# An output projection by Strassen's seven half products, and a small product in half-height tiles, in a fused attention and FFN kernel

## The chip, the cores and the metric

The kernel runs on one core of a Trainium2 chip. A core has TensorE (PE in the profile; its weight loads are PEld), VectorE (DVE), ScalarE (ACT), GpSimd (POOL), SyncE (SP, which issues every DMA of this kernel) and 16 DMA engines. The metric is the device time of one launch in microseconds (us), lower is better.

## The reference

Eight batches of x (8 heads, 512 tokens, 64 wide) attend to a state of 32 rows per head, and the state attends to x. Both results go through a two-layer network:

```python
xread = softmax(x @ state.T * scale) @ state          # 512 rows a batch
sread = softmax(state @ x.T * scale) @ x              # 32 rows a batch
x = concatenate([xread, sread], axis=2)               # 544 rows a batch, 512 wide
h = x @ w_in                                          # 512 -> 2048
g = h - tanh(h)
out = g @ w_out                                       # 2048 -> 512
```

## The kernel before

Names used below: a *chunk* is one batch's 512 token rows (chunks 0 to 7); chunk 8 is the 256 state rows of all batches together. The 2048 hidden columns are 16 blocks f of 128.

**Split products.** Every fp32 operand is kept as two rounded parts. `split` (L92) makes them: ScalarE copies the value into a rounded `hi`, VectorE subtracts to get `lo`. A product is then three matmuls: hi·hi, hi·lo, lo·hi.

**Hidden layer.** x itself never meets w_in: for each batch the kernel forms m = state @ w_in and multiplies the attention weights aT by it. `Chunk.hidden` makes one block f of 512 tokens: six matmuls (L392 to L394) into a PSUM bank of `ps_h`, which has two. `finish` applies tanh (ScalarE), then h - tanh (VectorE, one input in PSUM), which frees the bank, then `split` into a `g` tile.

**Output.** `Chunk.output` adds block f to four PSUM banks (`ps_o`, one for each 128 tokens), three matmuls of 512 columns each (L430 to L432): 12 matmuls for each f, 192 for each chunk. The weights w_out stay in on-chip memory as `wo`, all 16 blocks split. `hidden` runs two blocks (`LAG`) ahead of `output`, so a chunk is a strict alternation of 6 and 12 matmuls.

**Where m comes from.** For batches 0 and 1 `m_first_two` makes it. For batches 2 to 7 `m_units` does, beside the chunks: group g = 0 is batches 2 to 5, g = 1 batches 6 and 7. For each of 8 pairs of heads it splits the 64 rows of w_in of each head with a ScalarE copy and a VectorE subtract of 64 partitions (L186, L187), stacking hi and lo on top of each other so that one full-height matmul does two of the three terms. A head then takes two matmuls in g = 0 (L194, L195) and one in g = 1. The result goes to device memory and is loaded back (`load_m`) and split, 1024 columns at a time, when a chunk needs it.

**Beside it.** The attention of batch b runs as nine *units* (a generator), the last four of them the state read. Lists of step numbers say after which step which unit is emitted. A planner with a timeline model orders each engine's queue; each engine then executes its queue strictly in order. `tc.issue_after(x)` puts what is emitted inside it behind x on x's engine. A step is one (chunk, f).

**The start.** w_in and w_out come as 64-bit words and are converted on VectorE and ScalarE in chunk 0 (`Weight.steps`, L124 to L128).

Of the kernel before, what the change touches and what calls it, by code (L numbers as in the profile page):

```python
# [19 lines left out]
P = 128  # L20
# [13 lines left out]
@with_exitstack  # L34
def attention_ffn(ctx: ExitStack, tc: tile.TileContext, xT, xn, bd, bh, sp, sm, sl, win, wout, xout, sout):

# [17 lines left out]

    PB = int('3')
    WB = int('2')
# [4 lines left out]
    OB = int('2')  # L61
    RB = int('2')
    GB = int('3')
    TB = int('3')
    CB = int('2')
    RRB = int('1')
    PTB = int('2')
    ident = cpool.tile([P, P], F32, name="ident")
    make_identity(nc, ident)
    wo = cpool.tile([P, NFF, 2, DM], F32R, name="wo")  # L70
    sr = [cpool.tile([P, DM], F32, name=f"sr{g}") for g in range(2)]
# [15 lines left out]
    def twins(name, shape, dtype):  # L87
        return pool.tile(shape, dtype, tag="twins", name=name)

    raws = itertools.cycle([parts] * PB + [twins] * 2)  # L90

    def split(hi, lo, src, sub=None):  # L92

        nc.scalar.copy(hi, src)  # L94
        return (sub or nc.vector).tensor_sub(lo, src, hi)  # L95

    class Weight:
# [17 lines left out]
        def steps(self, dst):  # L115

            if self.src.dtype == F32:
                return [lambda: None] * 3 + [lambda: nc.gpsimd.tensor_copy(dst, self.raw)]
            low, high = self.raw[:, :, 0], self.raw[:, :, 1]
            u, i = dst.bitcast(U32), dst.bitcast(I32)  # L120
            r = pool.tile([P, 512], I32, tag="cr", name=f"{self.name}r", bufs=CB)
            return [

                lambda: nc.vector.tensor_scalar(u, high, 3, 0x3FFFFFFF, ALU.logical_shift_left, ALU.bitwise_and),  # L124
                lambda: nc.vector.scalar_tensor_tensor(u, high, 0xC0000000, u, ALU.bitwise_and, ALU.bitwise_or),  # L125

                lambda: nc.scalar.activation(r, low, AF.Copy, scale=2.0**-29),
                lambda: nc.vector.tensor_add(i, i, r),  # L128
            ]
# [18 lines left out]
    def second(q):  # L148
        if q < 2:
            return pool.tile([P, 2, 512], F32, tag="stage", name=f"mr1{q}", bufs=SB)  # L150
        return pool.tile([P, 2, 512], F32, tag=f"mr1{q}", name=f"mr1{q}", bufs=1)

# [12 lines left out]
    def m_units(g):  # L165
# [12 lines left out]
        for q in range(NQ):  # L178
            for k in range(2):
                w = pool.tile([P, 2, 512], F32, tag="wf", name=f"w1{g}{q}{k}", bufs=WB)  # L180
                nc.sync.dma_start(w, wf[q][:, 2 * k : 2 * k + 2])
                for c in range(2):
                    p = 2 * k + c

                    t = twins(f"wst{g}{q}{p}", [P, 2, 512], F32R)
                    split(t[0:64, 0], t[64:128, 0], w[0:64, c], WSUB)  # L186
                    split(t[64:128, 1], t[0:64, 1], w[64:128, c], WSUB)  # L187
                    hs = slice(2 * c, 2 * c + 2)
                    stage = pool.tile([P, 2, 512], F32, tag="stage", name=f"st{g}{q}{p}", bufs=SB)
                    for e in range(2):  # L190
                        h = 2 * p + e
                        ps = bank(ps_a, f"mps{g}{q}{h}")
                        if g == 0:
                            nc.tensor.matmul(ps, s[:, 1, h], t[:, e], start=True, stop=False)  # L194
                        nc.tensor.matmul(ps, s[:, 0, h], t[:, e], start=(g == 1), stop=True)  # L195
                        nc.scalar.copy(stage[:, e], ps)  # L196
# [38 lines left out]
    def convert_wout(f, part):  # L235
        w = pool.tile([P, 512], F32, tag="wor", name=f"wor{f}", bufs=RB)
        part.convert(w)
        split(wo[:, f, 0], wo[:, f, 1], w)


    def attention(b, aT):
# [34 lines left out]
        for hf in range(2):  # L276
            if b < LONE:
                scores(hf)
            ps = pss[hf]
            s = pool.tile([P, 512], F32, tag=f"s{b}{hf}" if b < EARLY_S else "s", name=f"s{b}{hf}", bufs=1 if b < EARLY_S else 2)  # L280
            nc.scalar.copy(s, ps)
# [26 lines left out]

    late = {}

# [59 lines left out]
    class Chunk:  # L370
# [9 lines left out]
        def hidden(self, f):  # L380
# [7 lines left out]
            for k in range(nk):  # L388
# [4 lines left out]
                nc.tensor.matmul(ps, mhi[k][:, cols], alo[:, k], start=False, stop=False)  # L393
                nc.tensor.matmul(ps, mlo[k][:, cols], ahi[:, k], start=False, stop=(k == nk - 1))  # L394
            self.finish(f, ps)

        def finish(self, f, ps):
            i, n = self.i, self.n
            t = pool.tile([P, 512], F32, tag="t", name=f"t{i}_{f}", bufs=TB)[:, :n]
            tanhs.append((nc.scalar.activation(t, ps, AF.Tanh).ins, nc.vector.tensor_sub(t, ps, t).ins))  # L400
# [26 lines left out]
        def add(self, f, t):  # L427
            g, o = self.g[f], self.o[t]
            tok = slice(t * P, t * P + P)
            nc.tensor.matmul(o, g[:, 0, tok], wo[:, f, 0], start=(f == 0), stop=False)  # L430
            nc.tensor.matmul(o, g[:, 0, tok], wo[:, f, 1], start=False, stop=False)  # L431
            return nc.tensor.matmul(o, g[:, 1, tok], wo[:, f, 0], start=False, stop=(f == NFF - 1)).ins  # L432

# [93 lines left out]
    def step(op):  # L527
# [7 lines left out]
        elif k == "c":  # L535
            ss[j] = pool.tile([P, 512], F32, tag=f"s0{j}", name=f"s0{j}", bufs=1)
            o(nc.scalar.copy(ss[j], sps_ps[j]))
# [113 lines left out]
    if "att0" in SCH:  # L651
        a2 = SCH.pop("att0")
        D0["att"]["1"] = [x for x in a2]
    D0.update(SCH)
    convs = iter([(1, 2), (1, 3)] + [(q, p) for q in (2, 3) for p in range(4)])
    pairs = iter([(1, 2), (1, 3)] + [(q, p) for q in (2, 3) for p in range(4)])
    wo_it = iter(range(1, NFF))
    for i in range(B + 1):
        for f in range(NFF):
# [10 lines left out]
            if nf < NFF:  # L670
                if nf % 4 == 0:
                    chunks[i].prepare(nf // 4)
                chunks[i].hidden(nf)
            elif i + 1 <= B:
                if nf == NFF:
                    if i + 1 == B:
                        turn_sread()
                    chunks[i + 1].prepare(0)
                chunks[i + 1].hidden(nf - NFF)
            for _ in range(D0["pair"].count(st)):  # L680
                m_first_two(*next(pairs))

            with ExitStack() as gates:
                if st < GATED:
                    for x in tanhs[st]:
                        gates.enter_context(tc.issue_after(x))
                advance(a0, D0["a0"].count(st))
                advance(late1, D0["r1"].count(st))
                for b in range(1, B):
                    n = D0["att"][str(b)].count(st)  # L690
                    if n:
                        if b not in atts:
                            atts[b] = new_attention(b)
                        advance(atts[b], n)
                for g in range(2):
                    advance(m1[g], D0[f"m{g}"].count(st))
            chunks[i].output(f)

# [48 lines left out]
```

## Time and profile before

| | |
|---|---|
| median of 3 runs | 683.47 us (683.39 to 683.52) |
| profiled execution | span 681.6 us from first to last instruction; its own launch time isn't given, the median stands 1.9 us above its span |
| PE busy | 97% of the span |
| VectorE, ScalarE, GpSimd busy | 67%, 56%, 1% |
| moved by DMA | 95.05 MB, mean 139 GB/s |
| first stores of chunk 0 | 130 us |

The span is from the first to the last instruction of one profiled execution. Busy time of PE counts a matmul from its start to its modelled end; matmuls overlap, so the distance between two starts is what one costs. A row of the timeline is start, duration, engine, line, operation, output<-input, shape.

### The profile page before, as it was taken

The page shows a single profiled execution, that of the slowest core. Times are in us where ns is not written, and L with a number is a line of the kernel's source. Part 1 is how long each engine was busy: PE and PEld are TensorE (multiplying, and loading weights), DVE is VectorE, ACT ScalarE, POOL GpSimd, SP SyncE. Part 2 cuts the span into 40 slices and gives each one's busy share as a digit, 9 for nine tenths or more (in the row PEclk, how much of TensorE's full clock was granted, in tenths as well). Part 3 has the DMA queues.
Part 4 walks back from the last instruction along what each step waited for, and adds up shares of the span by engine and source line. Part 5 has one row for each costly group of instructions (what it writes and reads, how often), then busy time and mean ns, then how long its engine had stood idle before and what let it go on. Part 6 is the DMA issues. An engine that isn't in the chain of part 4 may idle for free.

```text
span 681.6 us, 9389 instructions
## 1 busy us (share of the span) xinstructions
PE 657.8 (97%) x3458; PEld 518.4 (76%) x3458; DVE 457.4 (67%) x805; ACT 378.5 (56%) x667; POOL 3.8 (1%) x9
## 2 busy tenths in 40 slices
PE   5888989999999999999999999999999999999997
PEld 2555666788788878787888777887878788888896
DVE  5988999864966469756966488637854687434442
ACT  3878866866756546756756464635433354333342
POOL 2000000000000000000000000000000000000000
PEclk9789999999999999999999999999999999999999
DMA  8779840555536642735445333653241312001310
GB/s 297 202 277 332 279 154 18 174 154 149 189 94 190 167 158 67 243 95 183 129 155 156 124 128 110 200 186 128 93 162 54 124 37 100 21 14 44 129 32 31
DMA packets 43694, 95.05 MB, mean 139 GB/s; under 512 B 5888, under 2 KB 11264, under 8 KB 43648
## 3 DMA queue, kind: packets, MB, share of 16 engines
q1 hardware_dynamic: 43648, 94.46, 43.1%
q8 instruction: 27, 0.44, 0.3%
q14 instruction: 19, 0.16, 0.1%
HBM read 64.55 MB, written 29.88 MB: 139 GB/s over the span
## 4 chain that ended last, share of the span: by engine, by line
PE 81%; DVE 11%; DMA 4%; ACT 1%; issue 1%; SPq 0%; ACTq 0%; DVEq 0%
PE ops L430 16%; PE ops L432 16%; PE ops L431 16%; PE hps L392 8%; PE hps L393 8%; PE hps L394 8%; PE mps L195 2%; DVE t L400 1%; PE rps L346 1%; PE sps L270 1%; DVE wor L125 1%; PE pps L336 1%; DVE g L95 1%; DMA w01d<-in_win 1%; DMA wo2d<-in_wout 1%
## 5 line engine op out<-in xcount | busy, mean ns | idle before, releaser
L431 PE MATMUL ops<-wo,g 128*128 128x512 f32 x544 | 213.7, 393 | 4.5 <-DVE wo L95 4.5
L430 PE MATMUL ops<-wo,g 128*128 128x512 f32 x544 | 207.0, 395 | 0.6 <-ACT wo L94 0.5
L432 PE MATMUL ops<-wo,g 128*128 128x512 f32 x544 | 205.6, 391 | 0.0
L400 DVE TENSOR_TENSOR t<-hps,t 128x512 f32<-128x512 f32 (+1 forms) x142 | 93.7, 661 | 95.8 <-ACT t L400 95.1
L400 ACT ACTIVATE t<-hps 128x512 f32<-128x512 f32 (+1 forms) x142 | 81.6, 575 | 133.8 <-PE hps L394 130.0
L94 ACT CAST g<-t 128x512 fp32r<-128x512 f32 (+1 forms) x142 | 84.8, 598 | 73.7 <-DVE t L400 54.4
L431 PEld LDWEIGHTS ops<-wo,g 128*128 128x128 f32 x544 | 102.2, 188 | 28.8 <-DVE wo L95 7.5
L95 DVE TENSOR_TENSOR g<-t,g 128x512 fp32r<-128x512 f32 (+1 forms) x142 | 93.6, 660 | 45.0 <-ACT g L94 43.5
L430 PEld LDWEIGHTS ops<-wo,g 128*128 128x128 f32 x544 | 102.5, 189 | 27.9 <-ACT wo L94 3.0
L432 PEld LDWEIGHTS ops<-wo,g 128*128 128x128 f32 x544 | 102.0, 188 | 23.4 <-issue 1.3
L392 PE MATMUL hps<-aT,m 128*128 128x512 f32 x248 | 99.8, 403 | 1.2 <-DVE t L400 1.0
L394 PE MATMUL hps<-aT,m 128*128 128x512 f32 x248 | 96.6, 391 | 0.6 <-DVE m L95 0.5
L393 PE MATMUL hps<-aT,m 128*128 128x512 f32 x248 | 97.0, 391 | 0.0
L392 PEld LDWEIGHTS hps<-aT,m 128*128 128x128 f32 x248 | 46.6, 188 | 15.1 <-DVE t L400 2.2
L394 PEld LDWEIGHTS hps<-aT,m 128*128 128x128 f32 x248 | 46.6, 188 | 11.2 <-DVE m L95 1.5
L393 PEld LDWEIGHTS hps<-aT,m 128*128 128x128 f32 x248 | 46.6, 188 | 10.1 <-issue 1.0
L95 DVE TENSOR_TENSOR wst<-w,wst 64x512 fp32r<-64x512 f32 x64 | 43.9, 686 | 13.9 <-ACT wst L94 12.1
L196 ACT COPY st<-mps 128x512 f32<-128x512 f32 x64 | 36.3, 588 | 15.7 <-PE mps L195 14.1
L95 DVE TENSOR_TENSOR m<-mr,m 128x1024 fp32r<-128x1024 f32 x31 | 37.9, 1223 | 8.0 <-ACT m L94 7.8
L94 ACT CAST wst<-w 64x512 fp32r<-64x512 f32 x64 | 39.7, 620 | 0.8
L94 ACT CAST m<-mr 128x1024 fp32r<-128x1024 f32 x31 | 32.3, 1045 | 3.5 <-DMA mr<-md 2.8
L195 PE MATMUL mps<-wst,sms 128*128 128x512 f32 x64 | 24.9, 395 | 0.0
(215 smaller groups left out, 584.1 us busy)
## 6 DMA issues: line engine op xcount, KB each, us to landing
md<-st SPq DMA_DIRECT2D x128, 128.0 KB, 2.2
mr<-md SPq DMA_DIRECT2D x24, 512.0 KB, 4.0
xT<-in_xT SPq DMA_DIRECT2D x16, 512.0 KB, 4.1
w<-wf SPq DMA_DIRECT2D x16, 512.0 KB, 4.3
out_x<-ob SPq DMA_DIRECT2D x32, 256.0 KB, 2.1
xn<-in_xn SPq DMA_DIRECT2D x16, 512.0 KB, 3.5
wn<-wf SPq DMA_DIRECT2D x8, 512.0 KB, 4.1
ml<-md SPq DMA_DIRECT2D x8, 512.0 KB, 3.8
```

The costliest lines, as they stand in the source:

```text
L94: nc.scalar.copy(hi, src)
L95: return (sub or nc.vector).tensor_sub(lo, src, hi)
L125: lambda: nc.vector.scalar_tensor_tensor(u, high, 0xC0000000, u, ALU.bitwise_and, ALU.bitwise_or),
L195: nc.tensor.matmul(ps, s[:, 0, h], t[:, e], start=(g == 1), stop=True)
L196: nc.scalar.copy(stage[:, e], ps)
L392: nc.tensor.matmul(ps, mhi[k][:, cols], ahi[:, k], start=(k == 0), stop=False)
L393: nc.tensor.matmul(ps, mhi[k][:, cols], alo[:, k], start=False, stop=False)
L394: nc.tensor.matmul(ps, mlo[k][:, cols], ahi[:, k], start=False, stop=(k == nk - 1))
L400: tanhs.append((nc.scalar.activation(t, ps, AF.Tanh).ins, nc.vector.tensor_sub(t, ps, t).ins))
L430: nc.tensor.matmul(o, g[:, 0, tok], wo[:, f, 0], start=(f == 0), stop=False)
L431: nc.tensor.matmul(o, g[:, 0, tok], wo[:, f, 1], start=False, stop=False)
L432: return nc.tensor.matmul(o, g[:, 1, tok], wo[:, f, 0], start=False, stop=(f == NFF - 1)).ins
```

## The change

**Output of chunks 2 to 7.** They are taken in three pairs (2,3), (4,5), (6,7), and a new class `Pair` replaces `output` for them. Token rows a and b, even and odd f, and the two 256-column halves of w_out make a 2x2 by 2x2 block product; it is done with seven half products (m1 to m7 in the order of `ORDER`) and sums of blocks. Each half product has four steps j of 12 matmuls (weights: a 128x128 piece of w_out, moving: 512 tokens), so a pair takes 28 steps. The output comes out transposed and is stored to a new tensor `tout`.

- **Weights.** After chunk 0 and 1 `wo` isn't kept: `keep_row` writes its 16 blocks to device memory, `mix_rows` forms four sums of blocks on GpSimd, splits them and writes them too. `Pair.load` fetches the 512 KB for each step again: 84 loads. `load_rows` brings the 16 blocks back for chunk 8.
- **Operands.** h - tanh is kept unsplit in a tile `G`. Before a step `Pair.split` splits 1024 columns of it. `hidden_done` forms two sums for each j, on GpSimd for j 0 to 2 and on VectorE for j = 3. `Pair.split` adds one GpSimd subtraction for each step of m5 and m6.
- **Order.** For the first pair the hidden blocks of chunk 2 come four in a row between steps (ticks "H" and "P"), then those of chunk 3; in the other pairs first two H to one P. Then four P (m6), then 16 P, each followed by one H of the next chunk, except in the last pair, where they follow each other.
- **Sums.** `close` copies finished banks out (ScalarE) or adds a copy to them (VectorE).

**m of batches 2 to 7.** `m_units` splits both heads of a pair in one copy and one subtract of 128 partitions, and multiplies each head in a tile of 64 rows of the array, the two heads in turn: three terms a head in g = 0, two in g = 1.

**Around it.** Buffer counts and the lists of steps change (`ASIDE`, `SIDES`): attention 2 and m_units g = 0 sit in steps 15 to 27, eight `mix_rows` in steps 17 to 30.

```diff
+    def big(name, shape, dtype):
+        return pool.tile(shape, dtype, tag="big", name=name, bufs=BIG)   # BIG=16
...
 def m_units
-                    split(t[0:64, 0], t[64:128, 0], w[0:64, c], WSUB)
-                    split(t[64:128, 1], t[0:64, 1], w[64:128, c], WSUB)
+                    split(t[:, 0], t[:, 1], w[:, c])
...
+                    pss = [bank(ps_a, f"mps{g}{q}{2 * p + e}") for e in range(2)]
+                    terms = [(0, 0), (0, 1)] + [(1, 0)] * (g == 0)
+                    for n, (x, y) in enumerate(terms):
+                        for e in range(2):
+                            rows = slice(64 * e, 64 * e + 64)
+                            nc.tensor.matmul(
+                                pss[e], s[rows, x, 2 * p + e], t[rows, y], start=(n == 0), stop=(n == len(terms) - 1)
+                            )
...
 Chunk.finish
+            if 2 <= i < B:
+                if f % 4 < 2:
+                    self.g[f // 4, f % 2] = big(f"G{i}_{f}", [P, 2, 512], F32)
+                g = self.g[f // 4, f % 2][:, f % 4 // 2]
+                main(nc.scalar.activation(t, ps, AF.Tanh), nc.vector.tensor_sub(g, ps, t))
+                return
...
+    KEEP = [8 + x for x in range(16)]
+    MIX = [17 + 2 * x for x in range(7)] + [30]
...
+    def mix_rows(j):
+        a = parts(f"wa{j}", [P, 2, 2, 256], F32)
+        for e in range(2):
+            w = wo[2 * j + e].bitcast(F32)
+            nc.gpsimd.tensor_add(a[:, e].rearrange("p h n -> p (h n)"), w[:, 0], w[:, 1])
+        a11, a21, a12, a22 = a[:, 0, 0], a[:, 0, 1], a[:, 1, 0], a[:, 1, 1]
+        nc.gpsimd.tensor_add(a22, a21, a22)
+        nc.gpsimd.tensor_sub(a21, a11, a21)
+        nc.gpsimd.tensor_sub(a11, a22, a11)
+        nc.gpsimd.tensor_sub(a12, a12, a11)
+        src = a.rearrange("p e h n -> p (e h n)")
+        hl = [parts(f"ws{j}{k}", [P, 4, 256], F32R) for k in range(2)]
+        split(*(x.rearrange("p s n -> p (s n)") for x in hl), src)
+        for k in range(2):
+            nc.sync.dma_start(wsd[:, :, j // 2, j % 2, k], hl[k].bitcast(F32))
...
+    class Pair:
+        ORDER = ("m1", "m2", "m6", "m5", "m7", "m3", "m4")
+        def load(self):
...
+            w = parts(f"W{self.n}{k}{j}", [P, 2, 2, 256], F32R)            # "parts": 4 tiles
...
+            nc.sync.dma_start(w.bitcast(F32), src)
...
+        def split(self):
...
+            if k == "m5":
+                main(nc.gpsimd.tensor_sub(src, self.source("m3", j), src))
+            g = [pool.tile([P, 2, 512], F32R, tag="g", name=f"g{self.n}{k}{j}{c}", bufs=GB) for c in range(2)]
+            main(*split(*(x.rearrange("p f n -> p (f n)") for x in g), src))
+            if k == "m6":
+                b = self.source("m4", j)
+                main(nc.gpsimd.tensor_sub(b, b, src))
+
+        def hidden_done(self, f):
+            if f % 4 == 3:
+                j = f // 4
+                a, c, d = (self.source(k, j) for k in ("m6", "m7", "m3"))
+                eng = nc.vector if j == 3 else nc.gpsimd
+                main(eng.tensor_sub(c, d, c), eng.tensor_add(a, a, c))
+
+        def product(self):
...
+            for e in range(2):
+                for t in range(2):
+                    cols = slice(128 * t, 128 * t + 128)
+                    for c, (x, y) in enumerate(((0, hi), (0, lo), (1, hi))):
+                        made = nc.tensor.matmul(out[t], w[:, e, x, cols], y[:, e], ...)
...
+    for n, duo in enumerate(duos):
+        ticks, left, per = [], 8, 2
+        if n == 0:
+            for s in range(4):
+                ticks += [("H", a, f) for f in range(4 * s + 2, min(4 * s + 6, NFF))] + ["P"]
+            left, per = 4, 4
+        hs = [("H", b, f) for f in range(NFF)]
+        for s in range(left):
+            ticks.append("P")
+            ticks += hs[per * s : per * s + per]
+        ticks += ["P"] * 4
+        for s in range(16):
+            ticks.append("P")
+            if n < 2:
+                ticks.append(("H", b + 1, s))
...
+            if n == 2 and at >= len(ticks) - 14 and nrow < NFF:
+                load_rows(nrow)
```

More of the change, by code (lines that the diff above doesn't have):

```diff
@@ L307, in attention @@
             late[b] = ss
-    late = {}
+    late, kept = {}, {}
+    chain = [None]
     def late_read(b):
@@ L657, in attention_ffn, with keep_row, main, side @@
     wo_it = iter(range(1, NFF))
-    for i in range(B + 1):
+    def keep_row(f):
+        nc.sync.dma_start(wod[:, f % 2, f // 2], wo[f].bitcast(F32))
+    def mix_rows(j):
[13 more added lines that the diff above has]
+            nc.sync.dma_start(wsd[:, :, j // 2, j % 2, k], hl[k].bitcast(F32))
+    mains, NEAR = [[]], 8
+    def main(*made):
+        mains[-1].extend(x.ins for x in made)
+    late_units = {"a0": a0, "r1": late1, "m0": m1[0], "m1": m1[1]}
+    def side(name, n=1):
+        if not n:
+            return
+        if name[:3] == "att":
+            b = int(name[3:])
+            if b not in atts:
+                atts[b] = new_attention(b)
+            advance(atts[b], n)
+        else:
+            advance(late_units[name], n)
+    for i in range(2):
         for f in range(NFF):
@@ L683, in attention_ffn @@
             with ExitStack() as gates:
[L684 to L694, printed above, removed]
@@ L695, in attention_ffn @@
-                for g in range(2):
-                    advance(m1[g], D0[f"m{g}"].count(st))
-            chunks[i].output(f)
+                for x in tanhs[st]:
+                    gates.enter_context(tc.issue_after(x))
+                for name, at in ASIDE.items():
+                    side(name, at.count(st))
+                for x in range(KEEP.count(st)):
+                    keep_row(next(rows))
+                for x in range(MIX.count(st)):
+                    mix_rows(next(mixes))
@@ new lines, in load_rows, with hidden @@
+    def load_rows(f):
+        wo[f] = big(f"wl{f}", [P, 2, DM], F32R)
+        nc.sync.dma_start(wo[f].bitcast(F32), wod[:, f % 2, f // 2])
+    def hidden(c, f, own=None):
+        if f // 4 not in chunks[c].m:
+            chunks[c].prepare(f // 4)
+        chunks[c].hidden(f)
+        chunks[c].reached = f
+        if f % 4 == 2 and f < 12:
+            chunks[c].prepare(f // 4 + 1)
+        if own is not None:
+            own.hidden_done(f)
+    duos = [Pair(n, chunks[2 * n + 2], chunks[2 * n + 3]) for n in range(3)]
@@ new lines, in attention_ffn @@
+    for n, duo in enumerate(duos):
+        a, b = duo.a.i, duo.b.i
+        ticks, left, per = [], 8, 2
[12 more added lines that the diff above has]
+                ticks.append(("H", b + 1, s))
+        if n == 0:
+            for _ in range(3):
+                duo.load()
+        for at, tick in enumerate(ticks):
+            if tick == "P":
+                duo.load()
+                if duo.split_at == duo.at:
+                    duo.split()
+                duo.split()
+                with tc.issue_after(chain[0]):
+                    duo.product()
+                if n < 2 and duo.at >= 26:
+                    duos[n + 1].load()
+            else:
+                with tc.issue_after(chain[0]):
+                    hidden(tick[1], tick[2], duo if tick[1] == b else None)
+                if duo.split_at == duo.at:
+                    duo.split()
+            with ExitStack() as gates:
+                for x in [x for t in mains[-NEAR:-LAG] for x in t]:
+                    gates.enter_context(tc.issue_after(x))
+                for name, where in SIDES[n].items():
+                    side(name, where.count(at))
+            mains.append([])
+            if n == 2 and at == 8:
+                turn_sread()
+            if n == 2 and at >= len(ticks) - 14 and nrow < NFF:
+                load_rows(nrow)
+                nrow += 1
@@ L700 @@
+    for f in range(nrow, NFF):
+        load_rows(f)
+    last = chunks[B]
+    last.prepare(0)
+    with tc.issue_after(chain[0]):
+        for f in range(LAG):
+            last.hidden(f)
+    for f in range(NFF):
+        if f + LAG < NFF:
+            if (f + LAG) % 4 == 0:
+                last.prepare((f + LAG) // 4)
+            last.hidden(f + LAG)
+        last.output(f)
 def kernel(x, state, moe_w_in, moe_w_out):
```

166 lines of the change are left out of this document (137 added, 29 removed).

## Prediction

> **What bounds the kernel now.** I read the page's first lines, its 40 slices and the chain, then the busy times by stage.
>
> ```profile
> span 681.6 us, 9389 instructions
> PE 657.8 (97%) x3458; PEld 518.4 (76%) x3458; DVE 457.4 (67%) x805; ACT 378.5 (56%) x667; POOL 3.8 (1%) x9
> PE   5888989999999999999999999999999999999997
> DVE  5988999864966469756966488637854687434442
> PEclk9789999999999999999999999999999999999999
> PE 81%; DVE 11%; DMA 4%; ACT 1%; issue 1%; SPq 0%; ACTq 0%; DVEq 0%
> ```
>
> TensorE carries 81% of the chain. VectorE's 11% is the start. By stage (columns: stretch, its length, busy PE, PEld, DVE, ACT, POOL with counts, clock, DMA share, GB/s):
>
> ```profile
> 60.00:120.00 60.00, 56.25 (x236) 40.35 (x235) 59.75 (x104) 45.41 (x76) 0.00 (x0) 1.00 0.52 179
> 120.00:205.00 85.00, 84.31 (x415) 68.33 (x414) 59.31 (x99) 57.36 (x101) 0.00 (x0) 1.00 0.50 150
> 205.00:622.00 417.00, 416.72 (x2333) 333.72 (x2332) 270.33 (x477) 215.64 (x374) 0.00 (x0) 1.00 0.39 124
> ```
>
> To 120 us VectorE is full (59.75 of 60) and sets the pace; from there PE never rests, at granted clock 1.00, and VectorE is busy 70%, then 65%. So after about 120 us a matmul taken away is time taken away, as long as the other engines keep up. What one costs (here one period of the alternation, from its first matmul to the next period's first, 6 + 12 matmuls):
>
> ```profile
> 607.07 0.39 PE L392 MATMUL hps<-aT,m 128*128 128x512 f32 x1
> ...
> 611.15 0.39 PE L392 MATMUL hps<-aT,m 128*128 128x512 f32 x1
> ```
>
> 4.08 us for 18, so 0.227 us each: a hidden block (H) is 1.36 us, a step of 12 (P) 2.72 us.
>
> **The change part by part.** The sum is made against the span of 681.6; the median of the runs, 683.47, is 1.9 higher, and I carry that 1.9 to the end.
>
> *1. Products: -32.6 us.* Two chunks had 2 x 192 = 384 output matmuls, a pair has 28 x 12 = 336: 48 fewer, 144 in three pairs, all 128x128 by 512 as before. 144 x 0.227 = 32.6. They lie on the path (PE 417 of 417).
>
> *2. m_units on PE: +2 us (from -3.6 to +14.5).* g = 0 goes from 64 full matmuls to 96 half-height ones, g = 1 from 32 to 64. If the two heads run at once, 160 halves take 80 places instead of 96: -16 x 0.227 = -3.6. If not, 160 - 96 = 64 places more: +14.5. Before there are tiles of 64 rows in the scores:
>
> ```profile
> 172.35 0.39 PE L430 MATMUL ops<-wo,g 128*128 128x512 f32 x1
> 172.58 0.39 PE L431 MATMUL ops<-wo,g 128*128 128x512 f32 x1
> 172.90 1.09 PE L270 MATMUL sps<-xT,bdr 64*32 64x512 f32 x16
> 173.92 0.50 PE L432 MATMUL ops<-wo,g 128*128 128x512 f32 x1
> 174.25 0.39 PE L392 MATMUL hps<-aT,m 128*128 128x512 f32 x1
> ```
>
> Sixteen records, eight tiles in two row groups, are through in 1.02 us, less than five full matmuls: row groups do run at once. But going into the other shape took 0.32 us instead of 0.23, and coming back 0.33: 0.1 each way. In 32 groups of halves that is 32 x 0.2 = 6.4, so -3.6 + 6.4 = +2.8 if each group stays together; I take +2. [...]
>
> *3. VectorE and ScalarE.*
>
> ```profile
> L400 DVE TENSOR_TENSOR t<-hps,t 128x512 f32<-128x512 f32 x93 | 64.2, 691 | 76.0 <-ACT t L400 75.5
> L95 DVE TENSOR_TENSOR g<-t,g 128x512 fp32r<-128x512 f32 x92 | 63.3, 689 | 31.0 <-ACT g L94 30.5
> L95 DVE TENSOR_TENSOR m<-mr,m 128x1024 fp32r<-128x1024 f32 x22 | 26.9, 1223 | 7.5 <-ACT m L94 7.4
> L95 DVE TENSOR_TENSOR wst<-w,wst 64x512 fp32r<-64x512 f32 x38 | 26.1, 686 | 8.6 <-ACT wst L94 7.5 <-PE hps L394 0.3
> ```
>
> (These are of 205 to 622 us.) The subtractions of h - tanh stay. A pair's 32 splits of 512 (22 us) become 28 of 1024 (34 us); the sums of j = 3 add 2.4 and the closing adds take the place of copies. m_units halves its splits, -0.69 each of 32. Over the stretch: 270 + 3 x (12 + 2.4) - 19 x 0.69 = 300 us of VectorE for 417 - 33 = 384 of PE, 78% where it was 65%. The first pair is above the mean: two and a half attentions, two late state reads and 12 of 16 units of g = 1. Its PE is 28 x 2.72 + 46 x 1.36 = 139, some 160 us with the side work. Its VectorE is 46 x 0.69 + 28 x 1.22 + 11 m x 1.22 + 12 x 0.69 + about 55 of side work (all else in the window, 270 - 64 - 63 - 27 - 26 = 90 us for five attentions, reads and stores, so 13 to 18 an attention) = 143, 89%. That is throughput enough, since back to back these cost less than they last:
>
> ```profile
> 80.67 0.70 DVE L95 TENSOR_TENSOR wo<-wor,wo 128x512 fp32r<-128x512 f32 x1
> 81.28 0.70 DVE L289 TENSOR_TENSOR e<-e,m 128x512 f32<-128x512 f32 x1
> ...
> 88.09 1.24 DVE L95 TENSOR_TENSOR m<-mr,m 128x1024 fp32r<-128x1024 f32 x1
> 89.22 0.71 DVE L128 CUSTOM_DVE_ANT_0 wor<-wor,wo8r 128x1024 uint16<-128x1024 uint16 x1
> ```
>
> 0.61 and 1.13 us from start to start. Chunk 1 gets eight splits of mix_rows and four units of attention 3 on top of attention 2 and g = 0: 32 x 0.61 + 12 x 1.13 + 16 x 0.61 + about 19 = 62 us, beside 80 of PE. ScalarE adds 1.04 a split (592.87 below), 56% before; I cost it at nothing under VectorE's slack of the same steps, +3 if that cover goes. Cost of chunk 1 and of blocked turns in the pairs: +2 (0 to 20; the 20 is worked out under the rivals).
>
> *4. Four hidden blocks in a row: +3 us (2 to 12).* Two PSUM banks; a bank is free when tanh and subtraction are done:
>
> ```profile
> 587.80 0.39 PE L394 MATMUL hps<-aT,m 128*128 128x512 f32 x1
> 588.29 0.60 ACT L400 ACTIVATE t<-hps 128x512 f32<-128x512 f32 x1 [2.10 <-PE hps L394]
> 588.92 0.69 DVE L400 TENSOR_TENSOR t<-hps,t 128x512 f32<-128x512 f32 x1 [2.01 <-ACT t L400]
> ...
> 592.87 1.04 ACT L94 CAST m<-mr 128x1024 fp32r<-128x1024 f32 x1
> ```
>
> The last matmul gives way at 588.03, the bank is free at 589.61: 1.6 us, with both engines idle. Today 4 us lie between. In a burst of four, H(f) waits for the bank of H(f-2) with only 1.36 us between: 0.25 lost for each of 8 bursts, 2 us. One VectorE instruction of 1.13 in the way makes it 1.4, 11 us. Behind the waiting matmul stands all of PE. I take +3, near the idle end, since side matmuls can be queued there. With one P or more between, the slack is 4.1 us and costs nothing.
>
> *5. From m6 to m5: +4 us (0 to 14).* GpSimd's price:
>
> ```profile
> 8.95 1.16 POOL L545 TENSOR_TENSOR e<-e,m 128x512 f32<-128x512 f32 x1 [7.22 <-DVE m L543]
> 11.31 1.43 POOL L545 TENSOR_TENSOR e<-e,m 128x512 f32<-128x512 f32 x1 [1.20 <-DVE m L543]
> ```
>
> so 2.3 to 2.9 us for 1024. After the pair's last H: 1.6 to G, 2 x 1.13 for the sums of j = 3 (4 us), GpSimd's subtraction for m6 (6.4), that for m5 (8.7), ScalarE 1.04 and VectorE 1.2: 11.0 us until m5 can start; four P of m6 cover 10.9. That is even. After it each m5 step needs one GpSimd turn of 2.3: hidden in the first two pairs (P + H, 4.1 us), not in the last, where P is 2.7 and GpSimd and VectorE may also take turns (below): 8 x (2.33 + 1.13) - 8 x 2.72 = 6 us. I take 0.5, 0.5 and 3.
>
> *6. Transfers: +1 us (0 to 11).* 84 weight loads of 512 KB, 16 back, 32 writes: 69 MB more, on SP's queue with all others.
>
> ```profile
> 60.00:80.00 20.00, 20.00 (x92) 14.16 (x91) 20.00 (x35) 17.74 (x31) 0.00 (x0) 1.00 0.85 300
> w<-wf SPq DMA_DIRECT2D x16, 512.0 KB, 4.3
> L447 SPq DMA_DIRECT2D out_x<-ob x32: 332/338/704, 130.9 to 638.3; - x32
> ```
>
> An issue takes SP 0.34 us: 132 more are 45 us over some 550, free. 300 GB/s were moved at share 0.85. One load for each P in the densest place is 0.52 MB in 2.72 us, 193 GB/s, and three lie ahead (8 us) of a landing in 4.3. The keep and mix writes have steps 8 to 30, the stretch at share 0.5. Only in the last 14 steps does a block of w_out join each load: 14.7 MB in 38 us, 386 GB/s; at 300 that is 49 us, 11 more, of which three preloaded tiles hide 8 and rows that slip into chunk 8 the rest. A block also waits for a free G with the weight loads queued behind it on SP. I take +1.
>
> *7. Turn to chunk 8: +1.5 us (0 to 3).* Its first blocks now follow the last product instead of running beside it: one pass through tanh, subtraction and split, some 3 us, covered by half.
>
> Sum: -32.6 + 2 + 2 + 3 + 4 + 1 + 1.5 = -19.1. From 683.5: **664 us**. With these ends (all low: -34, all high: +33) I keep 656 to 673 for this case.
>
> **The rivals.**
>
> *A. GpSimd holds VectorE up.* The same place, about 12 us:
>
> ```profile
> 11.98 1.30 DVE L128 CUSTOM_DVE_ANT_0 w<-w,w00r 128x1024 uint16<-128x1024 uint16 x1
> ...
> 16.53 0.63 DVE L128 CUSTOM_DVE_ANT_0 w<-w,w01r 128x1024 uint16<-128x1024 uint16 x1
> ```
>
> While GpSimd worked from 11.31 to 12.74, a VectorE instruction with two inputs in on-chip memory lasted 1.30 and ended at 13.28, 0.54 after GpSimd; alone it lasts 0.63. So they took turns. Every `lo` subtraction is such an instruction, and the change brings 42 GpSimd operations of 1024 (98 us) and 8 x (2 x 1.16 + 4 x 0.6) = 38 us of mix_rows. In full alternation chunk 1 needs 62 + 38 = 100 us for 80 of PE, +20; the first pair 124 (its 143 at the back-to-back price) + 33 = 157 for 160, but its bursts find VectorE late, +9 over my 3; the last pair +3. 664 + (20 - 2) + 9 + 3 = 694, slower. It decides once more than 19 us beyond my sum are lost, about 14% of GpSimd's 136 us. Against it: VectorE has 20% to spare and subtractions from PSUM have one such input. [...]
>
> *B. All of it hidden.* Side matmuls fill the bursts, halves pair, GpSimd is early: 683.5 - 32.6 - 3.6 + 3 = 650.
>
> *C. Halves don't pair* or their groups are torn apart, as L195 is today by matmuls of other products: +14.5 instead of +2: 676.
>
> *D. The reloads starve PE in the last pair and SP's order delays loads in the first:* +11 and another 3 instead of +1: 677.
>
> **How the numbers follow.** Forecast 0.45 (656 to 673), B 0.18 (645 to 656), C 0.10, D 0.10, A 0.17, of which 0.14 beyond 0.2% slower and 0.03 within. 0.2% (1.4 us) is about what a measurement of this kernel tells from no change. Faster 0.83, same 0.03, slower 0.14. The range takes in B, C and D and leaves out A: 646 to 685.
>
> **What would show it.** Right: matmuls of the new product at 0.227 us, 1008 of them; PE's share at 93 to 96%; PE idle in chunk 2 on the subtraction of h - tanh, and between m6 and m5 on VectorE's split. The GpSimd operations at 2.3 to 2.9 us, and the splits beside them at 2 us and more where they overlap. Halves of 64 rows starting in twos within 0.1 us. Wrong: PE idle in sum over 35 us after 120 us (A), halves 0.2 us apart (C), PE waiting for a DMA of W (D). A VectorE at 95% or more through chunk 1 and the first pair would mean A.

## The result and the profile after

The changed kernel takes 732.4 us (730.96 to 733.29, 4 runs) against 683.43: ratio 1.0715, interval 1.07 to 1.0731. That is slower, where 664 was forecast, and outside the range.

The page of the changed kernel: its span, the busy times, PE, GpSimd and the granted clock in 40 slices, and the chain's share by engine.

```profile
span 731.3 us, 9639 instructions
...
PE 670.3 (92%) x3378; PEld 497.3 (68%) x3378; DVE 565.5 (77%) x781; ACT 399.3 (55%) x643; POOL 183.1 (25%) x99
...
PE   4899879999989798778999999788999999799997
...
POOL 2000034755500025722000006563000069600000
PEclk9899999999999999998999999989999999999999
...
PE 54%; DVE 28%; DMA 7%; issue 6%; ACT 2%; POOL 2%; SPq 0%; ACTq 0%; DVEq 0%; POOLq 0%
```

PE's row has three dents after the start, and POOL's row has its three later humps at about the same slices. Before, PE stood at 9 from the seventh slice on, and VectorE carried 11% of the chain; now it carries 28%. The windows by stage say it in numbers (columns as in the prediction). The first row is chunk 1, the others are the three pairs, each cut where m6 ends:

```profile
134.00:213.00 79.00, 77.77 (x419) 57.50 (x417) 55.79 (x81) 44.19 (x77) 37.61 (x32) 1.00 0.86 281
213.00:336.00 123.00, 102.75 (x519) 71.33 (x520) 105.01 (x140) 64.53 (x104) 37.72 (x14) 0.92 0.56 177
336.00:421.50 85.50, 85.50 (x515) 61.27 (x515) 58.39 (x104) 52.60 (x83) 0.00 (x0) 0.99 0.77 241
421.50:503.00 81.50, 72.37 (x383) 52.97 (x382) 74.84 (x83) 41.01 (x63) 40.15 (x14) 0.92 0.69 225
503.00:572.60 69.60, 69.60 (x371) 55.07 (x371) 52.33 (x76) 35.99 (x51) 0.08 (x1) 0.99 0.65 207
572.60:640.00 67.40, 61.66 (x265) 49.70 (x265) 57.92 (x43) 31.78 (x43) 42.24 (x14) 0.97 0.48 150
640.00:682.00 42.00, 41.65 (x184) 33.98 (x183) 20.32 (x20) 15.77 (x18) 0.00 (x0) 1.00 1.01 383
```

In the pairs PE is full where GpSimd rests (second, fourth and last part), and loses 20, 9 and 6 us where GpSimd works. The last row moves 383 GB/s and PE is still full: the reloads are not what it waits for. Chunk 1 (first row) has as much GpSimd work and loses hardly anything. Three things differ there: no sum stands between a hidden block and a product, products alternate with hidden blocks, and VectorE is busy 71% of the stage, where it is 85%, 92% and 86% of the pairs' first parts. Those shares are averages. In windows of 20 us VectorE is full, or nearly, where PE runs dry:

```profile
300.00:320.00 20.00, 15.80 (x88) 10.93 (x87) 18.64 (x25) 8.40 (x16) 11.43 (x5) 0.91 0.49 159
440.00:460.00 20.00, 20.00 (x100) 14.54 (x100) 20.00 (x19) 13.37 (x21) 13.16 (x5) 1.00 0.80 248
460.00:480.00 20.00, 14.50 (x55) 10.44 (x53) 20.00 (x21) 6.01 (x10) 11.43 (x5) 0.91 0.60 204
```

At first PE still finds work (440 to 460 us), then it waits. In chunk 1 VectorE is full for 20 us as well (160 to 180), and PE does not wait. Which of the three differences decides there was not tried.

What happens in a dent, from the timeline (GpSimd, then VectorE, then PE):

```profile
303.60 5.84 POOL L841 TENSOR_TENSOR G<-G,G 128x1024 f32<-128x1024 f32 x2
309.52 2.34 POOL L834 TENSOR_TENSOR G<-G,G 128x1024 f32<-128x1024 f32 x1
...
309.60 2.81 DVE L312 TENSOR_TENSOR e<-e,z 128x512 f32<-128x512 f32 x1
312.44 0.69 DVE L419 TENSOR_TENSOR G<-hps,t 128x512 f32<-128x512 f32 x1
...
318.80 0.69 DVE L312 TENSOR_TENSOR e<-e,z 128x512 f32<-128x512 f32 x1
...
313.18 0.74 PE L405 MATMUL hps<-aT,m 128*128 128x512 f32 x1 [3.29 <-DVE G L419]
313.72 0.63 PE L406 MATMUL hps<-aT,m 128*128 128x512 f32 x1
314.15 0.63 PE L407 MATMUL hps<-aT,m 128*128 128x512 f32 x1
```

VectorE's L312 belongs to an attention and has nothing to do with the pair. It starts 0.08 us after a GpSimd subtraction and ends 0.55 after it: 2.81 us, where the same instruction takes 0.69 at 318.80. Behind it in VectorE's queue stands the subtraction L419 that frees the bank of a hidden block. It lasts only 0.69 (one of its inputs is in PSUM; the 21 of its kind that overlap a GpSimd instruction last 0.67 to 0.69), but it comes late, and PE has waited 3.29 us. The next matmuls then start 0.43 apart instead of 0.227: the granted clock has dropped to 0.50, of which more at the end.

The groups show the same as averages; this holding up of VectorE by GpSimd is called the lock below (GpSimd, then VectorE; columns: count, busy us, mean ns, idle before):

```profile
L841 POOL TENSOR_TENSOR G<-G,G 128x1024 f32<-128x1024 f32 x18 | 53.8, 2987 | 287.6 <-DVE G L419 286.9
...
L828 POOL TENSOR_TENSOR G<-G,G 128x1024 f32<-128x1024 f32 x12 | 32.7, 2725 | 23.4 <-DVE g0m L99 10.9 <-DVE g1m L99 7.6 <-DVE nm L338 3.7
...
L99 DVE TENSOR_TENSOR m<-mr,m 128x1024 fp32r<-128x1024 f32 x31 | 51.2, 1653 | 1.3 <-ACT m L99 1.1
```

The split of m took 1223 ns before and takes 1653 on average now. Summed over every VectorE instruction that overlaps a GpSimd one, against the median of those of its kind that don't, VectorE is held up by about 80 us, some 20 of them beside mix_rows, which e1 below keeps.

PE's largest group of waits from 205 to 640 us, after (columns: us, times, longest):

```profile
PE hps L405 <- DVE G L419: 13.3, 9, 3.3
```

and the only one of before:

```profile
PE hps L392 <- DVE t L400: 0.3, 1, 0.3
```

For a load of W, PE waited once in the changed kernel, 0.3 us at 671 us.

Followed back along the releasers that the profile infers, to the last matmul on the chain, about 29 of the 47.3 us of PE's gaps (counted as below) have at least as much held-up time of VectorE behind them; sums on GpSimd stand on the chain of two gaps, 4.9 us. This is a reading of the trace, not an experiment.

### The profile page after: what moved, and what is told of

It is laid out like the page before. It is cut to its first block, busy times and chain, and to the rows that moved or that the text cites. A ratio compares the mean times of both kernels' runs of the same rounds, so it can differ in the third digit from the quotient of the medians.

```text
span 731.3 us, 9639 instructions
## 1 busy us (share of the span) xinstructions
PE 670.3 (92%) x3378; PEld 497.3 (68%) x3378; DVE 565.5 (77%) x781; ACT 399.3 (55%) x643; POOL 183.1 (25%) x99
## 4 chain that ended last, share of the span: by engine, by line
PE 54%; DVE 28%; DMA 7%; issue 6%; ACT 2%; POOL 2%; SPq 0%; ACTq 0%; DVEq 0%; POOLq 0%
PE X L861 15%; PE hps L405 5%; PE hps L406 5%; PE hps L407 5%; PE Y0m L861 4%; DVE m L99 4%; PE mps L198 3%; PE Y1m L861 3%; PE ops L452 3%; PE ops L453 3%; PE ops L454 3%; DVE G L419 2%; PE Y2m L861 2%; POOL G L841 2%; DVE wst L99 1%
## 5 line engine op out<-in xcount | busy, mean ns | idle before, releaser
L841 POOL TENSOR_TENSOR G<-G,G 128x1024 f32<-128x1024 f32 x18 | 53.8, 2987 | 287.6 <-DVE G L419 286.9
L405 PE MATMUL hps<-aT,m 128*128 128x512 f32 x248 | 103.3, 417 | 18.4 <-DVE G L419 13.3
L419 DVE TENSOR_TENSOR G<-hps,t 128x512 f32<-128x512 f32 x96 | 64.9, 683 | 33.0 <-ACT t L419 32.7
L419 ACT ACTIVATE t<-hps 128x512 f32<-128x512 f32 x96 | 56.9, 597 | 57.1 <-PE hps L407 57.0
L99 DVE TENSOR_TENSOR g2m<-G,g2m 128x1024 fp32r<-128x1024 f32 x28 | 45.6, 1636 | 20.1 <-PE Y2m L861 7.8
L861 PE MATMUL X<-g0m,W0m 128*128 128x512 f32 x192 | 53.2, 421 | 6.5 <-ACT g0m L99 4.2
L453 PE MATMUL ops<-wo,g 128*128 128x512 f32 x128 | 51.3, 405 | 4.0 <-DVE wo L99 4.0
L99 DVE TENSOR_TENSOR m<-mr,m 128x1024 fp32r<-128x1024 f32 x31 | 51.2, 1653 | 1.3 <-ACT m L99 1.1
L861 PE MATMUL X<-g1m,W1m 128*128 128x512 f32 x192 | 50.0, 406 | 2.1 <-DVE g1m L99 2.1
L861 PE MATMUL X<-g2m,W2m 128*128 128x512 f32 x192 | 47.1, 401 | 4.9 <-ACT g2m L99 2.8
L454 PE MATMUL ops<-wo,g 128*128 128x512 f32 x128 | 49.9, 395 | 0.0
L99 DVE TENSOR_TENSOR g1m<-G,g1m 128x1024 fp32r<-128x1024 f32 x28 | 39.5, 1416 | 12.4 <-PE X L861 7.3
L99 DVE TENSOR_TENSOR g0m<-G,g0m 128x1024 fp32r<-128x1024 f32 x28 | 38.2, 1366 | 12.2 <-ACT g0m L99 9.2
```

The lines of the kernel that those rows point to most:

```text
L99: return nc.scalar.copy(hi, src), (sub or nc.vector).tensor_sub(lo, src, hi)
L405: nc.tensor.matmul(ps, mhi[k][:, cols], ahi[:, k], start=(k == 0), stop=False)
L419: main(nc.scalar.activation(t, ps, AF.Tanh), nc.vector.tensor_sub(g, ps, t))
L453: nc.tensor.matmul(o, g[:, 0, tok], w[:, 1], start=False, stop=False)
L454: return nc.tensor.matmul(o, g[:, 1, tok], w[:, 0], start=False, stop=(f == NFF - 1)).ins
L841: main(eng.tensor_sub(c, d, c), eng.tensor_add(a, a, c))
```

## The experiments

A count used throughout: PE's *gaps* are the distances between two matmul starts above 0.45 us, less 0.227 each, summed after 120 us. Before has 4.7 us of them, the changed kernel 47.3.

**e1_fill: GpSimd keeps its time but reads nothing.** In the changed kernel each of GpSimd's 42 sums is left out and becomes three fills of the same tile.

```diff
-                main(nc.gpsimd.tensor_sub(src, self.source("m3", j), src))
+                for v in range(3):
+                    main(nc.gpsimd.memset(src, 0.25 * v))
```

> Left out: GpSimd's 42 sums in the pairs; each is replaced by three GpSimd fills of the same tile, which write it and read nothing. Dependencies on GpSimd and about 3 us of its time for each stay. Lock theory (GpSimd's reads and VectorE's two-input instructions take turns): VectorE's splits of 1024 beside GpSimd fall from 2 to 3 us to 1.2, VectorE's busy time from 565 to about 505 us, PE's idle time after 213 us from 41 to under 20, half-clock windows mostly go; 732 becomes 675 to 695. Rival (PE waits for GpSimd's own 3 us a sum and for the order of the queues, not for the lock): VectorE's rows fall, the time stays at 720 to 732.

Measured: 688.0 us, 1.0056 (1.0028 to 1.0084). Its busy times on the page:

```profile
PE 654.3 (95%) x3378; PEld 488.5 (71%) x3378; DVE 506.1 (74%) x781; ACT 400.2 (58%) x643; POOL 182.2 (26%) x183
```

and its groups of the fills and of the split of m:

```profile
L784 POOL MEMSET G<- 128x1024 f32 x126 | 119.0, 955 | 282.8 <-ACT g1m L99 96.7 <-DVE g2m L99 84.4 <-DVE g0m L99 72.1
...
L99 DVE TENSOR_TENSOR m<-mr,m 128x1024 fp32r<-128x1024 f32 x31 | 39.3, 1270 | 2.7 <-PE rps L359 1.8 <-ACT m L99 0.8
```

GpSimd is as busy as in the changed kernel (182.2 against 183.1), and VectorE's 781 instructions take 506.1 us where they took 565.5. 44.4 us of the 49 are gone, and PE's gaps fall to 14.9. So GpSimd's busy time by itself is not the loss. But the run takes out two things. GpSimd no longer holds VectorE (the 28 splits of the last pair, g2m, average 1223 ns, where they took 1636 in the changed kernel), and a fill does not wait for the second operand: the fills wait for the split that read their tile (the first row above), the sums waited for a hidden block (L419 in the row of L841). In the first pair the fills run from 219.7 to 318.6 us, the sums of the changed kernel from 269.8 to 335.1, so unlike what was expected not every dependency on GpSimd stayed. 44.4 us is the price of both together. That most of it is the holding rests on VectorE's 59 us and on the chains above, with 4.9 us behind GpSimd's own sums; no run takes out the one without the other.

**e2_dve: all 42 sums on VectorE.**

```diff
-                main(nc.gpsimd.tensor_sub(b, b, src))
+                main(nc.vector.tensor_sub(b, b, src))
...
-                eng = nc.vector if j == 3 else nc.gpsimd
+                eng = nc.vector
```

> All sums of the pairs on VectorE (42 more of 1.13 to 1.2 us there), mix_rows stays on GpSimd. Lock theory: VectorE gives back about 60 us of waiting and takes up 50 us of work; what goes is the chain through GpSimd (2.9 us a sum becomes 1.2) and single blocks of 3 us: 695 to 715. Rival, VectorE simply has too much to do: no better than 732, PE still idle on VectorE.

Measured: 709.86 us, 1.0386 (1.0358 to 1.0414). It is in the range expected, and wins back half of what e1 does: the lock is gone from the pairs, but 42 x 1.22 = 51 us more stand in VectorE's queue, and PE's gaps are still 34.1 us. Rows of its timeline (VectorE, then PE):

```profile
302.52 0.68 DVE L890 TENSOR_TENSOR ob0m<-Y0m,s0m 128x512 f32<-128x512 f32 x1
303.12 1.22 DVE L99 TENSOR_TENSOR g0m<-G,g0m 128x1024 fp32r<-128x1024 f32 x1
304.25 0.69 DVE L890 TENSOR_TENSOR ob0m<-Y0m,s0m 128x512 f32<-128x512 f32 x1
304.85 1.22 DVE L840 TENSOR_TENSOR G<-G,G 128x1024 f32<-128x1024 f32 x1
305.98 0.69 DVE L419 TENSOR_TENSOR G<-hps,t 128x512 f32<-128x512 f32 x1
...
306.72 0.50 PE L405 MATMUL hps<-aT,m 128*128 128x512 f32 x1 [2.05 <-DVE G L419]
```

Each is at its clean duration, but the subtraction that frees the bank is fifth in a back-to-back row. The window of the stretch:

```profile
207.00:328.00 121.00, 106.28 (x572) 73.73 (x571) 96.36 (x152) 66.36 (x108) 0.00 (x0) 0.93 0.60 196
```

VectorE is busy 96 of 121 us, 80%, but its load is not even: from 255 to 270 us it is busy 8.67 of 15 us and PE 14.95, from 285 to 300 us it is 14.86 and PE 12.68. PE waits where VectorE is full, though the stage on average is not.

**e3_munits and e4_full160: the half-height tiles by themselves.** e3 is the kernel before with the new `m_units` alone. e4 is the same with the 160 matmuls at full height, so that no shape switches.

```diff
# e4 against e3
-                                pss[e], s[rows, x, 2 * p + e], t[rows, y], start=(n == 0), stop=(n == len(terms) - 1)
+                                pss[e], s[:, x, 2 * p + e], t[:, y], start=(n == 0), stop=(n == len(terms) - 1)
```

> The kernel before with the new m_units alone. By the changed kernel's records a group of six halves costs about 0.1 us more than four full matmuls and one of four costs 0.3 to 0.7 more than two: 16 x 0.1 + 16 x 0.5 = 10 us slower, 690 to 694, less a few where VectorE sets the pace (it saves 32 x 0.6 us). My prediction's +2.8 would give 686. If halves pair without cost: 680.

> The kernel before with the new m_units of 160 matmuls, but each of full height (128 rows), so no shape switch; each product then mixes the two heads of a pair (computed wrongly). Theory (a change between 64-row and 128-row matmuls costs about 0.4 us a group, and one head's halves run one after the other): 160 - 96 = 64 matmuls more by 0.227 = 14.5, so 698, faster than the 710 with halves though every matmul is twice as high. Rival (the halves' cost is their number or the new order of splits and copies): no better than 710.

Measured: e3 710.4 us, 1.0394 (1.0365 to 1.0423), 16 us above the range expected; e4 695.22, 1.0169 (1.0147 to 1.019), near the 698 of its theory. In the profile of e3, PE stays full: it is PE's own time that has grown. A group of three in e3, and one of six in the changed kernel:

```profile
160.45 0.39 PE L433 MATMUL ops<-wo,g 128*128 128x512 f32 x1
160.76 0.96 PE L194 MATMUL mps<-wst,sms 64*128 64x512 f32 x3
161.66 0.50 PE L434 MATMUL ops<-wo,g 128*128 128x512 f32 x1
```

```profile
129.94 0.39 PE L407 MATMUL hps<-aT,m 128*128 128x512 f32 x1
130.26 0.97 PE L198 MATMUL mps<-wst,sms 64*128 64x512 f32 x6
131.16 0.50 PE L405 MATMUL hps<-aT,m 128*128 128x512 f32 x1
131.49 0.39 PE L406 MATMUL hps<-aT,m 128*128 128x512 f32 x1
```

Six halves of two heads last as long as three of one: row groups do run at once. But from the full matmul ahead of the group of six to the second behind it is 1.55 us, where two full matmuls and three places would be 1.14: 0.4 us for each group, twice the 0.2 forecast. And the planner took most groups apart: of e3's 53 groups 24 have three matmuls (one head) and 14 have two. Together e3's halves cost 50.2 us where the 96 full ones cost 96 x 0.227 = 21.8: 28 more, and 27 were measured. e4 has the same number of matmuls at twice the height and is 15 us faster: in the groups that the planner made, halves cost that much more than full matmuls.

**e5_fill_oldm, e6_dve_oldm, e7_oldm: the old `m_units` back** in e1, e2 and the changed kernel.

> Fills in place of GpSimd's sums in the pairs (those left out, as in e1_fill) and the m_units of the kernel before. Theory (lock and half-height tiles are the two whole reasons): 688 - 25 = 663, up to 672 since VectorE and ScalarE get 20 us of splits back. Rival (something else in the pairs, bursts or transfers, holds it): above 678.

> Pair sums on VectorE, m_units of before; nothing left out. The two effects add: 710 - 25 = 685; VectorE's 20 us of extra splits may cost up to 8: 685 to 693. Rival (VectorE is the bound, PE work hides behind it): 705 or more.

> The changed kernel with the m_units of before, sums on GpSimd. 732 - 25 = 707, with 20 us more of VectorE work in stages where GpSimd blocks it: 707 to 717. Rival (m_units only costs where PE sets the pace, in the changed kernel it hides in PE's waits): 725 to 732.

Measured: 690.02 us, 1.0081 (1.0052 to 1.0111); 712.87, 1.0421 (1.0393 to 1.0449); 733.66, 1.0734 (1.071 to 1.0758). All three theories missed, and the rivals have the times (e7 just above its 732). So 27 us alone come to nothing in company, three times. In e7 against the changed kernel, chunk 1 and the second part of the first pair, both with next to no gaps, are 3.3 and 10.0 us shorter with the old units. But their 32 more VectorE instructions make chunk 0 8.1 us longer (137.4 against 129.3) and the first part of the first pair 5.6: 13.3 won, 13.7 lost. The new `m_units` are worth as much to VectorE's queue as they cost PE.

**e8_sides: side work moved away.** e2 with the four state-read units of batch 0 and the first four units of m1 behind m6 of the first pair.

```diff
-            "a0": [22, 25, 29, 31],
+            "a0": [56, 59, 62, 65],
...
-            "m1": list(range(24, 72, 4)),
+            "m1": [42, 44, 46, 48, 50, 52, 54, 58, 62, 66, 70, 72],
```

> Pair sums on VectorE as in e2_dve; the four late read units of batch 0 and the first four m_units of g = 1 move from the first pair's ticks 22 to 36 (up to its m6) behind them, where VectorE is busy 65 of 83 us. Nothing left out. Theory (VectorE is full up to m6 of the first pair, 100% from 270 to 330 us in e2_dve, so every us of work there is a us of time): 8 to 10 us of VectorE work leave the stage, so 710 becomes 700 to 703, the stage shorter by as much. Rival (the order of hidden blocks and their two banks holds PE there): within 2 us of 710.

Measured: 711.3 us, 1.0412 (1.0391 to 1.0434). The time is the rival's. The stage it was taken from is 8.9 us shorter (111.7 against 120.6), as the theory had it, but PE's own work there fell by more (94.1 us busy against 106.3), and its gaps stay. The first part of the second pair wins 5.6 and the second part loses 11.3 (77.8 against 66.5, with 7.9 us of gaps where e2 has none); why is not shown. PE's gaps sum to 34.7, as in e2's 34.1. So less load in the stage did not mean less waiting. This does not refute that VectorE is the bound there: of the last 50 us of the stage (270 to 320) it is still busy all but 0.3.

**e9_two_pairs and e10_one_pair: fewer pairs.** Strassen for chunks 4 to 7, and for 6 and 7 alone, with the old `m_units`, all sums on VectorE, the mixing of w_out spread over more chunks and the lists of side units moved to fit.

```diff
# e9
-    duos = [Pair(n, chunks[2 * n + 2], chunks[2 * n + 3]) for n in range(3)]
+    duos = [Pair(n, chunks[2 * n + 4], chunks[2 * n + 5]) for n in range(2)]
# e10
+    duos = [Pair(n, chunks[2 * n + 6], chunks[2 * n + 7]) for n in range(1)]
```

> Nothing left out: Strassen for two pairs only, (4,5) and (6,7); chunks 0 to 3 as in the kernel before, m_units of before, pair sums on VectorE, mix_rows spread over chunks 1 to 3 where VectorE has slack. Theory: 2 x 48 x 0.227 = 21.8 us less PE work, 5 to 10 lost at m6 to m5 and in the first pair, 3 at the turn to chunk 8, 2 to 5 beside mix_rows: 668 to 680, faster than before. Rival (a pair costs more than it saves wherever it stands): 690 or more.

> Strassen for one pair alone (chunks 6 and 7), where hardly any attention is left beside it (half of item 7's); m_units as before the change, sums on VectorE, the eight mixings of w_out spread over chunks 1 to 5, attention and state units of chunks 0 to 5 at their places of the kernel before. Nothing is left out. Theory (the products' saving is there, 28.7 us over three pairs, so 9.6 for one, and what eats it is VectorE's queue where attention, state units and sums meet ahead of the sixth product): here VectorE has the room, PE idles under 6 us beyond the kernel before, and the time is 674 to 682 us. Rival (a pair's own chain of hidden blocks, sums and splits starves PE whatever stands beside it, as the 17.8 us in the first pair with the sums on VectorE): PE idles 10 us or more in the pair's first part and the time is 684 or more.

Measured: e9 693.03 us, 1.0134 (1.0112 to 1.0157), with 26.4 us of gaps; e10 685.24, 1.0027 (1.0015 to 1.004), with 13.2. Both times miss the theory's range and lie where the rival put them. In the pair's first part e10's PE idles 8.3 us, between the theory's under 6 and the rival's 10 or more. The busy times on e10's page:

```profile
PE 648.6 (95%) x3410; PEld 506.6 (74%) x3410; DVE 512.8 (75%) x827; ACT 396.1 (58%) x675; POOL 59.5 (9%) x57
```

and the windows of its pair up to the last hidden block, and of the last 20 us of that:

```profile
503.00:580.00 77.00, 70.18 (x360) 53.91 (x359) 67.39 (x88) 40.59 (x61) 0.00 (x0) 1.00 0.42 137
560.00:580.00 20.00, 17.85 (x76) 13.77 (x76) 19.97 (x23) 9.27 (x14) 0.00 (x0) 1.00 0.32 106
```

PE works 9.2 us less than before (648.6 against 657.8): the saving of one pair is there. PE's gaps are 8.5 us more (13.2 against 4.7): it is eaten whole, with the attention nearly gone, no GpSimd sum in the pair, and the clock at 1.00. VectorE is busy 88% of the first part, and full at its end.

**e11_one_dve_mix: half an attention two steps later.**

```diff
-        "att7": [90, 92, 93, 95],
+        "att7": [92, 93, 94, 95],
```

> As e10_one_pair, but the second half of item 7's attention starts two steps later in chunk 5 (units at ticks 92 to 95 of the chunks' count instead of 90, 92, 93 and 95), so nearer to the pair. Theory: the same time within 2 us, as VectorE has room in chunk 5 and the pair's first part both. Rival: a later attention delays the hidden blocks of chunk 7, 2 us or more slower than e10_one_pair.

Measured: 684.6 us, 1.0012 (0.9997 to 1.0027), the same as e10 within 0.7 us, as the theory had it. It is also not told apart from the kernel before.

**e12_spread: the load of e10 spread out.** The hidden blocks of chunk 7 go between seven quarter products by twos and threes, and three quarters of m6 stand among them instead of behind them. The four subtractions for m4 stand with the splits of m5, and the turn of the state read comes at tick 44 instead of 26.

```diff
-        for s in range(left):
-            ticks.append("P")
-            ticks += hs[per * s : per * s + per]
-        ticks += ["P"] * 4
+        for per in (2, 2, 2, 2, 3, 3, 2):
+            ticks += ["P"] + hs[:per]
+            hs = hs[per:]
+        ticks += ["P"]
```

> e10_one_pair with VectorE's load ahead of the sixth product spread out: the sixteen hidden blocks of chunk 7 stand between seven quarter products by twos and threes instead of between four by fours, and the four later subtractions for m4 are issued with the splits of m5 instead of with those of m6. The same instructions, nothing left out. Theory (a hidden block's read-out stands in VectorE's queue behind sums of 1.22 us each, and PE waits for its bank): the gaps of PE after 120 us fall from 13.2 us (before: 4.7) to 6 to 9, and the time is 678 to 682 us, faster than the kernel before. Rival (the gaps come from the split that each quarter product needs just ahead of it, which the new order brings no earlier): gaps 12 us or more, 684 us or more.

Measured: 700.58 us, 1.025 (1.0227 to 1.0273): 15 us slower than e10, with gaps of 24.3. The theory missed. The rival's marks (gaps of 12 us or more, 684 us or more) are met, but it had no reason for the gaps to grow from 13.2. A window of it:

```profile
580.00:600.00 20.00, 10.02 (x31) 6.92 (x30) 13.98 (x15) 5.39 (x8) 0.00 (x0) 0.77 0.22 70
```

and the longest gap in its timeline (PE, VectorE, ScalarE):

```profile
593.85 0.39 PE L405 MATMUL hps<-aT,m 128*128 128x512 f32 x1
600.32 1.22 PE L851 MATMUL X<-g0m,W0m 128*128 128x512 f32 x2 [6.08 <-ACT g0m L99]
...
594.97 0.69 DVE L417 TENSOR_TENSOR G<-hps,t 128x512 f32<-128x512 f32 x1 [0.67 <-ACT t L417]
595.69 1.23 DVE L831 TENSOR_TENSOR G<-G,G 128x1024 f32<-128x1024 f32 x1
596.84 1.22 DVE L99 TENSOR_TENSOR wm<-wn,wm 128x1024 fp32r<-128x1024 f32 x1
597.97 1.22 DVE L831 TENSOR_TENSOR G<-G,G 128x1024 f32<-128x1024 f32 x1
...
599.23 2.94 ACT L99 CAST g0m<-G 128x1024 fp32r<-128x1024 f32 x3 [3.35 <-DVE G L831]
```

VectorE is at 70% and PE at half. The quarter product needs the hidden block's subtraction, two sums and the cast of the split, one after the other. A split of the next chunk's weights (wm) has slipped in between. The chain lasts 6 us, and PE, with its queue in order, starts no other matmul in that time (593.85 to 600.32). In e10 m6 stands behind all hidden blocks, so that the sums of its first quarters can be done by the time it comes up in PE's queue; in e12 PE meets each quarter's chain by itself. So here it is the length of the chain and the order of the queues that cost, not the sum of VectorE's work.

## Why the prediction was wrong, point by point

**The step that failed is "That is throughput enough" in part 3**, and with it "VectorE has 20% to spare" against rival A. By them the holding of VectorE stood in the sum within the 2 us of part 3, and A got a chance of 0.17. The lock itself was read from the trace of before (1.30 us beside GpSimd, 0.63 alone), and the GpSimd operations lasted about what was forecast (2725 to 2987 ns; 2.3 to 2.9 us). Both sentences judge VectorE by its mean load over a pair, without the time for which it is held. The load bunches up ahead of m6: from 460 to 480 us VectorE is busy 20.00 of 20 us and PE 14.50. e1 against the changed kernel prices the holding, together with the wait for a second operand, at 44.4 us. Of A's two signs, "PE idle in sum over 35 us" came (47.3 us of gaps). The other, VectorE at 95% through chunk 1 and the first pair, did not (71% and 85%), because it too was put as an average.

**A itself was mis-sized and put in the wrong place.** It gave chunk 1 20 us and the pairs 12, 694 in all. Chunk 1 lost next to nothing of PE (77.77 of 79.00), and nearly all lay in the pairs ahead of m6. There each held-up instruction delays a subtraction that frees a bank, or a sum that a product waits for. A counted VectorE's time over whole stages; what counted was where it is full and who stands behind the held instruction.

**The ends of the terms were added wrong.** All high gives 74.5 - 32.6 = +42, not +33. That is 725, still under the 732 measured.

**Part 1, right in kind, 4 us high.** From start to start, gaps and half clock left out, the 1008 product matmuls took 236.6 us and the 1152 they replace 265.3: -28.7, not -32.6. e10 shows -9.2 for one pair as PE's busy time.

**Part 2, mis-sized too.** +2 forecast, +27 alone: 0.4 us a group instead of 0.2, and groups torn into one head each, which is what rival C had. The upper end, 14.5, was too low as well, since it counted places and nothing for a group in the torn case. That it cost nothing net in the changed kernel fits VectorE's relief (e7), which the forecast had in its sum but not as time.

**Parts 4 and 5, near in sum where GpSimd does no sums, and in part elsewhere.** e10's pair has the bursts of the first pair and the close end of the last, so +3 and +3. Its waits are 3.5 us for a bank, none from m6 to m5, and 2.9 for the splits of products ahead of m6. In the changed kernel, too, PE loses nothing from m6's last matmul to m5's first (0.2 to 0.4 us from start to start); what it loses lies ahead of that. e1's gaps are 10.2 us above before, against the 7 forecast, but its fills skip a part of the chain. With the sums on either engine for real, they are 29 (e2) and 43 (the changed kernel).

**Part 6, right.** 383 GB/s in the densest stretch with PE full, and 0.3 us of waiting for a W: rival D is refuted.

**Part 7, too high.** In e10, from the last product to the last matmul it is 45.5 us against 42.6, and two hidden blocks (2.7 us) of chunk 8 have moved there from chunk 7: about nothing.

**Not in the prediction at all:** the half clock behind the gaps, below.

How the 49 us come together: products -28.7, gaps +42.6, half clock up to +19. The remaining 16 are near the 13.3 us that the new `m_units` take of PE in the stages without gaps. This is a sum of readings, not an experiment for each term; e1's 44.4 is measured, and lies in both gaps and half clock (e1: 32.4 us fewer gaps, and 6.8 us at half clock instead of 37).

**What stays open.** How much of e1's 44.4 us is the lock alone was not isolated. No order of the pair that keeps PE fed was found: e10 and e11 only come level with the kernel before, and no version beat it. Whether other work on PE during the chain (hidden blocks of chunk 8, say) would make one pair pay was not tried.

## What to carry to other kernels

An engine with an in-order queue is not judged by its mean load over a stage. Look for the stretch in which its load bunches up, and ask there of each instruction that frees a bank or feeds a product how many others can be ahead of it, and how long they last when held. Moving work to GpSimd beside VectorE was no free ride here: 120 us of it held VectorE for some 60, and 44 us came back when GpSimd filled tiles instead of adding them. A saving in matmuls that puts a chain of element-wise steps between two products needs other matmuls to run during that chain, or PE gives the saving back (9.2 us saved, 8.5 idle in e10).

## What the runs showed of the hardware

In the changed kernel PE's clock dropped behind gaps of PE's own. Two neighbouring windows of the changed kernel, just after the 3.29 us wait shown above:

```profile
313.30:316.70 3.40, 3.40 (x9) 2.15 (x9) 2.29 (x5) 0.60 (x2) 0.00 (x0) 0.50 0.35 98
316.70:320.10 3.40, 3.40 (x17) 2.63 (x15) 3.29 (x5) 3.40 (x7) 1.07 (x1) 1.00 0.20 72
```

Granted 0.50 for 3.4 us, and 9 matmuls instead of 17. Between 200 and 725 us this happens nine times (seven times for 3.4 us and twice for 6.8, 37 us in all, so up to 19 us lost), in e1 twice (6.8 us; granted 0.97 from 207 to 330 us), before never. The longest gap just ahead was 2.3 to 3.5 us in the changed kernel, but not each such gap did it: of two gaps of 2.3 us there, the one that ends at 254.3 us brought 3.4 us at 0.50 and the one that ends at 280.3 left the clock at 1.00, as did one of 2.2 us in e10. What decides it was not shown.

An instruction of VectorE with one input was held, too: in the same dent, a `TENSOR_SCALAR` over 128x16 took 2.36 us (it averages 568 ns in the changed kernel, 233 in e1). The prediction had counted two-input instructions alone.

```profile
304.65 2.36 DVE L310 TENSOR_SCALAR z<-z 128x16 f32<-128x16 f32 x1
```
